# The first two row tiles of x: transposed by a DMA queue instead of by TensorE

## The chip, the core and the metric

The kernel runs on one core of one Trainium2 chip. The metric is the device time of one execution in microseconds (us); lower is better. Three executions of the kernel before are listed, and one more was recorded by the hardware profiler. In that recording PE is TensorE (its weight loads are listed apart as PEld), ACT is ScalarE, DVE is VectorE, POOL is GpSimd, and SP is SyncE, which here only issues DMAs.

## What is computed

```python
def reference(x, w1, b1, w2):          # x 1x2048x512, w1 512x1792, b1 1792, w2 1792x512, all bfloat16
    h = jnp.einsum("bsd,df->bsf", x, w1) + b1
    sp = jnp.log1p(jnp.exp(-jnp.abs(h))) + jnp.where(h > 0, h, jnp.zeros_like(h))
    act = h * jnp.tanh(sp)
    return jnp.einsum("bsf,fd->bsd", act, w2)
```

It is a two-layer dense network with the Mish activation in between: `act(x @ w1 + b1) @ w2`.

## The kernel before

The 2,048 rows of x are worked off in four blocks of 512 rows. For each block a first product (line 177, written `mm1` here) makes h transposed, with one PSUM bank for each tile of 128 columns of w1 (an f tile, 14 of them), and four matmuls for each f tile, one for each 128-wide slice k of the inner dimension. ScalarE applies bias and Mish in one instruction (line 160), writing `a_sb`. The second product (line 199, `mm2`) makes 128 output rows at a time from 14 matmuls; VectorE copies them out of PSUM (line 205) and SP issues the store (line 208). Each engine's instruction order is written out by hand; a `Stream` object inserts a wait for a semaphore only where the engine has not waited for that value yet.

`mm1` needs x with its inner dimension on the partitions, the tile `xT`. The later three blocks get it from a DMA that transposes on its way (the helper `load` with `transpose=True`, line 85). For the first block two ways are used. Row tiles 0 and 1 (256 rows) come by a plain DMA into `x_nat`, row 2p in the first and row 2p+1 in the second half of partition p, and TensorE transposes them against an identity matrix (line 147), eight 128x128 transposes into four PSUM banks. VectorE and ScalarE copy two banks each into `xT` (line 151). GpSimd makes the identity (lines 120 and 122). Row tiles 2 and 3 come by a transposing DMA.

The order of the DMAs is this. ScalarE's queue issues w1's f tiles 0-3 in two halves, k 0-1 and k 2-3 (256 KB each). SP's queue issues `x_nat`, the transposing DMA of tiles 2-3, w1's f tiles 4-7 in two halves, b1, the rest of w1, w2, and the three transposing DMAs of the later blocks. b1 is turned on VectorE (lines 241, 243), and the first Mish waits for it.

Ahead of its work TensorE runs dummy matmuls on constants, whose numbers of columns are in `WARM` (line 130, 3,456 columns in all). Then come the transposes, then `first(...)`, which works on f tiles 0-3 of the first block: tile 0 alone with k 0, tile 1 alone with k 0, both with k 1 to 3, and then row tiles 2-3 with all k. Then `half` runs f tiles 4-7, k 0-1 and k 2-3, with the Mish of f tiles 0-3 queued behind the first half; then f tiles 8 to 13 follow, and the second product of the block.

Since row 2p+j is in column p of tile j, the stores of the first two output tiles go to every second row (`rows`).

Of the kernel before, what the change touches and what calls it, by code (L numbers as in the profile page):

```python
# [4 lines left out]

P = 128
SQ = 32
WARM = (512,) * 5 + (256,) * 3 + (128,)
BLOCKS = (512, 512, 512, 512)


# [21 lines left out]
def bass_standalone__dense_activation_mish__prompt_kernel(  # L33
# [6 lines left out]
):  # L40
    dt = mybir.dt
    ACT = mybir.ActivationFunctionType
    ALU = mybir.AluOpType
    BF, F32 = dt.bfloat16, dt.float32

    _, S, D = x.shape
    F = w1.shape[1]
    KT, FT = D // P, F // P
    assert (S, D, F) == (2048, 512, 1792) and sum(BLOCKS) == S
    x2, out2 = x[0], out[0]  # L50
# [4 lines left out]
    N0 = BLOCKS[0] // P  # L55

    with ExitStack() as es:
        def sb(name, shape, t):
            return es.enter_context(nc.sbuf_tensor(name, shape, t))

        x_nat = sb("x_nat", [P, 2, D], BF)
        xT = sb("xT", [P, KT, S], BF)
        w1_sb = sb("w1_sb", [P, KT, F], BF)
        w2_sb = sb("w2_sb", [P, FT, D], BF)
        b1_nat = sb("b1_nat", [SQ, P], BF)
        b1_T = sb("b1_T", [P, SQ], BF)
        b1_sb = sb("b1_sb", [P, FT], F32)
        ones = sb("ones", [P, P], BF)
        ident = sb("ident", [P, P], BF)
        a_sb = sb("a_sb", [P, FT, S], BF)  # L70
        o_sb = sb("o_sb", [P, S // P, D], BF)
        ps = es.enter_context(nc.psum_tensor("ps", [P, 8, 512], F32))

        def sem(name):
            return es.enter_context(nc.semaphore(name))

        sp = Stream(nc.sync, None)
        pe = Stream(nc.tensor, sem("c_pe"))
        dve = Stream(nc.vector, sem("c_dve"))
        act = Stream(nc.scalar, sem("c_act"))  # L80
        pool = Stream(nc.gpsimd, sem("c_pool"))

        def load(q, dst, src, name, transpose=False):
            s = sem(name)
            (q.eng.dma_start_transpose if transpose else q.eng.dma_start)(dst, src).then_inc(s, 16)
            return (s, 16)
# [8 lines left out]
        def load_part(q, k0, k1, a, b):  # L95
            t = load_w1(q, slice(k0, k1), a, b)
            for f in range(a, b):
                for k in range(k0, k1):
                    t_w1[k, f] = t

        t_bz = dve.mark(nc.vector.memset(b1_nat[:, :], 0.0))  # L101
        for k0, k1 in ((0, 2), (2, 4)):
            load_part(act, k0, k1, 0, F0)
        t_xn = load(sp, x_nat[:, :, :], x2[0:2 * P, :].rearrange("(p j) d -> p j d", p=P), "s_xn")
        t_x23 = load(sp, xT[:, :, 2 * P:4 * P], x2[2 * P:4 * P, :], "s_x23", True)
        for k0, k1 in ((0, 2), (2, 4)):
            load_part(sp, k0, k1, F0, 8)
        sp.wait(t_bz)
# [2 lines left out]
        t = load(sp, w2_sb[:, :, :], w2v, "s_w2")  # L111
# [3 lines left out]
        for s in range(1, len(BLOCKS)):  # L115
            lo, hi = starts[s], starts[s + 1]
            t_xT.append(load(sp, xT[:, :, lo:hi], x2[lo:hi, :], "s_xT%d" % s, True))


        t_ones = pool.mark(pool.eng.memset(ones[:, :], 1.0))  # L120
        pool.wait(t_ones)
        t_id = pool.mark(pool.eng.affine_select(ident[:, :], ones[:, :], pattern=[[1, P]], compare_op=ALU.is_equal,  # L122
                                                fill=0.0, base=0, channel_multiplier=-1))
        act.eng.preload_act_table(ACT.Mish)  # L124

        c_w = nc.const_aps.tensor(1.0, [P, P], BF)
# [2 lines left out]
        def dummy(n):  # L129
            nc.tensor.matmul(ps[:, 7, 0:n], c_w, c_m[:, 0:n], start=True, stop=True)  # L130


        free = [[] for _ in range(8)]
        t_cp = {(j, k): t_x23 for j in (2, 3) for k in range(KT)}
        t_mish, t_acc = {}, {}

        def transpose_x():

            pe.wait(t_xn, t_id)
            for bank, (eng, js, ks) in enumerate(((dve, (0,), (0,)), (act, (1,), (0,)), (dve, (0, 1), (1,)),  # L140
                                                  (act, (0, 1), (2, 3)))):
                n, m = len(ks), len(js)
                psb = ps[:, bank, 0:n * m * P // 2].bitcast(BF)
                for i, k in enumerate(ks):
                    for h, j in enumerate(js):
                        lo = (i * m + h) * P
                        mm = nc.tensor.transpose(psb[:, lo:lo + P], x_nat[:, j, k * P:(k + 1) * P], ident[:, :])  # L147
                eng.wait(pe.mark(mm))
                dst = xT[:, ks[0]:ks[0] + n, js[0] * P:(js[-1] + 1) * P]
                src = psb.rearrange("p (k t) -> p k t", k=n)  # L150
                t = eng.mark(nc.vector.tensor_copy(dst, src) if eng is dve else act.eng.activation(dst, src, ACT.Copy))  # L151
                for k in ks:
                    for j in js:
                        t_cp[j, k] = t
                free[bank] = [t]

        def mish(s, f, bank, t_mm):
            n = BLOCKS[s]
# [6 lines left out]
        def mm1_step(s, f, k, bank, js=None):  # L165

            n = BLOCKS[s]
            lo, hi = (0, n) if js is None else (js[0] * P, (js[-1] + 1) * P)
            first = k == 0 and lo == 0
            if first:  # L170
                pe.wait(*free[bank])
            pe.wait(t_w1[k, f])
            if s:
                pe.wait(t_xT[s])
            else:
                pe.wait(*[t_cp[j, k] for j in (js or range(N0))])
            return nc.tensor.matmul(ps[:, bank, lo:hi], w1_sb[:, k, f * P:(f + 1) * P],  # L177
                                    xT[:, k, starts[s] + lo:starts[s] + hi], start=first, stop=(k == KT - 1 and hi == n))

        def mm1(s, f, bank):  # L180
            for k in range(KT):
                mm = mm1_step(s, f, k, bank)
            mish(s, f, bank, pe.mark(mm))

        s_out = sem("s_out")
        n_out = 0

        def rows(i):

            if i < 2:  # L190
                return out2[0:2 * P, :].rearrange("(p j) d -> p j d", p=P)[:, i, :]
            return out2[i * P:(i + 1) * P, :]

        def mm2_step(i, f, lo, hi, bank):
            s = max(b for b in range(len(BLOCKS)) if starts[b] <= i * P)
# [6 lines left out]
        def put(i, lo, hi, bank, t_mm):  # L202
            nonlocal n_out
            dve.wait(t_mm)
            t = dve.mark(nc.vector.tensor_copy(o_sb[:, i, lo:hi], ps[:, bank, 0:hi - lo]))  # L205
            free[bank] = [t]
            sp.wait(t)
            sp.eng.dma_start(rows(i)[:, lo:hi], o_sb[:, i, lo:hi]).then_inc(s_out, 16)
            n_out += 1

        def mm2(i, lo, hi, bank):
            for f in range(FT):
                mm = mm2_step(i, f, lo, hi, bank)
            put(i, lo, hi, bank, pe.mark(mm))


        def first(js, ks):
            for k in ks:
                for f in range(F0):
                    mm = mm1_step(0, f, k, 4 + f, js)  # L220
                    if k == KT - 1 and js[-1] == N0 - 1:
                        t_acc[f] = pe.mark(mm)

        def half(fs, ks):
            for f in fs:
                for k in ks:
                    mm = mm1_step(0, f, k, f - F0)
                if ks[-1] == KT - 1:
                    t_acc[f] = pe.mark(mm)

        for n in WARM:
            dummy(n)
        transpose_x()
        first((0,), (0,))
        first((1,), (0,))
        first((0, 1), range(1, KT))
        first((2, 3), range(KT))

        dve.wait(t_b1)
        for j in range(P // SQ):  # L240
            t = dve.mark(nc.vector.transpose(b1_T[j * SQ:(j + 1) * SQ, :], b1_nat[:, j * SQ:(j + 1) * SQ]))  # L241
# [52 lines left out]
```

## Time and profile before

| | us |
|---|---|
| three executions, median (lowest to highest) | 105.17 (104.74 to 105.78) |
| the profiled execution, whole | 105.42 |
| its span, from the first instruction to the last | 104.1 |
| TensorE matmuls busy in the span | 101.5 (97%) |
| ScalarE busy | 39.7 (38%) |
| VectorE busy | 12.8 (12%) |

The profiled execution has 1.3 us outside its span. Times in views of the trace count from the span's start. A matmul's recorded duration holds its way through the array, and neighbours overlap; what a matmul costs in a row of matmuls is the distance between two starts.

### The profile page before, as it was taken

What the parts mean: (1) busy time and instruction counts of PE and PEld (TensorE: products, weight loads), DVE (VectorE), ACT (ScalarE), POOL (GpSimd) and SP (SyncE); (2) the same over time, 40 slices, a digit from 0 to 9 for tenths busy, and PEclk for the clock granted to TensorE, in tenths of its full rate; (3) what the DMA queues carried; (4) which work ended last, traced back from release to release, by engine and by line L of the source; (5) the groups of instructions that cost most, each with busy time, mean ns of one, the idle gap of its engine ahead of it and who ended that gap; (6) DMA issues with size and microseconds to landing.
All of it is one profiled execution on the core that took longest, in us unless ns stands there. A gap on an engine that the chain in (4) does not pass through costs nothing.

```text
span 104.1 us, 1139 instructions
## 1 busy us (share of the span) xinstructions
PE 101.5 (97%) x499; PEld 48.8 (47%) x499; DVE 12.8 (12%) x25; ACT 39.7 (38%) x59; POOL 0.7 (1%) x6
## 2 busy tenths in 40 slices
PE   6999999999999999999999999999999999999992
PEld 2786444444444444444444444444444444444462
DVE  0103000022220000022220000022112000011223
ACT  3405997000027777200007777500005777700000
POOL 2000000000000000000000000000000000000000
PEclk9999999999999999999999999999999999999999
DMA  2999999681101000010111000001111000001111
GB/s 46 334 339 363 348 317 178 145 203 50 44 7 50 0 0 6 0 50 0 50 50 50 0 0 3 0 6 50 50 50 50 0 0 0 0 0 57 50 50 50
DMA packets 13345, 7.94 MB, mean 76 GB/s; under 512 B 7836, under 2 KB 13212, under 8 KB 13340
## 3 DMA queue, kind: packets, MB, share of 16 engines
q1 hardware_dynamic: 12796, 7.35, 27.1%
q10 hardware_dynamic: 544, 0.52, 1.4%
q8 instruction: 4, 0.07, 0.3%
q14 instruction: 1, 0.01, 0.0%
HBM read 3.94 MB, written 2.10 MB: 58 GB/s over the span
## 4 chain that ended last, share of the span: by engine, by line
PE 97%; DVE 0%; issue 0%
PE ps L177 47%; PE ps L199 46%; PE ps L130 3%; PE ps L147 1%; DVE o_sb L205 0%
## 5 line engine op out<-in xcount | busy, mean ns | idle before, releaser
L160 ACT ACTIVATE a_sb<-ps,b_sb 128x512 bf16<-128x512 f32 x56 | 37.5, 691 | 48.0 <-PE ps L177 48.0
L177 PE MATMUL ps<-xT,w_sb 128*128 128x512 bf16 (+2 forms) x244 | 49.8, 367 | 0.0
L199 PE MATMUL ps<-w_sb,a_sb 128*128 128x512 bf16 (+2 forms) x238 | 49.0, 366 | 0.0
L177 PEld LDWEIGHTS ps<-xT,w_sb 128*128 128x128 bf16 x244 | 24.2, 101 | 24.8
L199 PEld LDWEIGHTS ps<-w_sb,a_sb 128*128 128x128 bf16 x238 | 22.8, 98 | 25.9
L205 DVE CAST o_sb<-ps 128x512 bf16<-128x512 f32 (+2 forms) x17 | 11.2, 660 | 82.4 <-PE ps L199 82.4
L130 PE MATMUL ps<-const-bfloat16-1.0 128*128 128x512 bf16 (+2 forms) x9 | 3.0, 519 | 0.8 <-PEq L279 0.8
L130 PEld LDWEIGHTS ps<-const-bfloat16-1.0 128*128 128x128 bf16 x9 | 1.2, 138 | 2.3 <-issue 2.2
L124 ACT ACT_TABLE_LOAD x1 | 1.3, 1283 | 1.8 <-issue 1.8
L151 ACT ACTIVATE xT<-ps 128x128 bf16<-128x128 bf16 (+1 forms) x2 | 0.9, 437 | 1.4 <-PE ps L147 1.4
L241 DVE STREAM_TRANSPOSE b_T<-b_nat 32x32 bf16<-32x32 bf16 x4 | 0.8, 202 | 3.3 <-DMA b_nat<-in_b_dram 3.2
L147 PE MATMUL ps<-ident,x_nat 128*128 128x128 bf16 x8 | 1.0, 311 | 0.0
L151 DVE COPY xT<-ps 128x128 bf16<-128x128 bf16 (+1 forms) x2 | 0.5, 258 | 3.2 <-PE ps L147 3.1
L147 PEld LDWEIGHTS ps<-ident,x_nat 128*128 128x128 bf16 x8 | 0.8, 142 | 0.2 <-DMA x_nat<-in_x_dram 0.2
L122 POOL TENSOR_SCALAR_AFFINE_SELECT ident<-ones 128x128 bf16<-128x128 bf16 x1 | 0.3, 292 | 0.1
L101 DVE MEMSET b_nat<- 32x64 uint32 x1 | 0.1, 112 | 0.9 <-PEq L279 0.9
L120 POOL MEMSET ones<- 128x128 bf16 x1 | 0.2, 204 | 0.3 <-POOLq L279 0.3
L243 DVE CAST b_sb<-b_T 128x14 f32<-128x14 bf16 x1 | 0.2, 176 | 0.0
L279 POOL MEMSET const-bfloat16-1.0<- 128x1 bf16 x1 | 0.1, 101 | 0.0
L279 POOL MEMSET const-uint8-127<- 128x1 uint8 x1 | 0.1, 101 | 0.0
L279 POOL MEMSET const-float32-0.0<- 128x1 f32 x1 | 0.1, 98 | 0.3 <-issue 0.3
L279 POOL MEMSET const-float32-1.0<- 128x1 f32 x1 | 0.1, 99 | 0.0
## 6 DMA issues: line engine op xcount, KB each, us to landing
out_dram<-o_sb SPq DMA_DIRECT2D x15, 128.0 KB, 1.7
w_sb<-in_w_dram SPq DMA_DIRECT2D x1, 1792.0 KB, 10.3
w_sb<-in_w_dram SPq DMA_DIRECT2D x1, 768.0 KB, 5.5
w_sb<-in_w_dram ACTq DMA_DIRECT2D x2, 256.0 KB, 3.8
w_sb<-in_w_dram SPq DMA_DIRECT2D x2, 256.0 KB, 4.4
x_nat<-in_x_dram SPq DMA_DIRECT2D x1, 256.0 KB, 2.9
out_dram<-o_sb SPq DMA_DIRECT2D x1, 96.0 KB, 1.6
xT<-in_x_dram SPq DMA_TRANSPOSE x4, 5.9
```

Source lines behind the costliest of these rows:

```text
L120: t_ones = pool.mark(pool.eng.memset(ones[:, :], 1.0))
L122: t_id = pool.mark(pool.eng.affine_select(ident[:, :], ones[:, :], pattern=[[1, P]], compare_op=ALU.is_equal, fill=0.0, base=0, channel_mu ...
L124: act.eng.preload_act_table(ACT.Mish)
L130: nc.tensor.matmul(ps[:, 7, 0:n], c_w, c_m[:, 0:n], start=True, stop=True)
L147: mm = nc.tensor.transpose(psb[:, lo:lo + P], x_nat[:, j, k * P:(k + 1) * P], ident[:, :])
L151: t = eng.mark(nc.vector.tensor_copy(dst, src) if eng is dve else act.eng.activation(dst, src, ACT.Copy))
L160: t = act.mark(act.eng.activation(a_sb[:, f, starts[s]:starts[s + 1]], ps[:, bank, 0:n], ACT.Mish, bias=b1_sb[:, f:f + 1]))
L177: return nc.tensor.matmul(ps[:, bank, lo:hi], w1_sb[:, k, f * P:(f + 1) * P], xT[:, k, starts[s] + lo:starts[s] + hi], start=first, stop=( ...
L199: return nc.tensor.matmul(ps[:, bank, 0:hi - lo], a_sb[:, f, i * P:(i + 1) * P], w2_sb[:, f, lo:hi], start=(f == 0), stop=(f == FT - 1))
L205: t = dve.mark(nc.vector.tensor_copy(o_sb[:, i, lo:hi], ps[:, bank, 0:hi - lo]))
L241: t = dve.mark(nc.vector.transpose(b1_T[j * SQ:(j + 1) * SQ, :], b1_nat[:, j * SQ:(j + 1) * SQ]))
L279: nc = _bacc.Bacc("TRN2", target_bir_lowering=False, num_devices=1)
```

## The change

Row tiles 0 and 1 of x are loaded by a transposing DMA straight into `xT`, as the first transfer of SP's queue; row tiles 2 and 3 by a second one behind it. What served the TensorE way goes: `x_nat`, the identity and its two GpSimd instructions, eight transposes, four copies, the every-second-row stores. The dummies are seven of 512 columns, one of 256 and two of 128 (4,096 columns). Tiles 0 and 1 are no longer taken singly for k 0, so `first((0, 1), range(KT))` has sixteen matmuls of 256 columns, where before eight of 128 and twelve of 256 stood. ScalarE's queue is as before.

```diff
-WARM = (512,) * 5 + (256,) * 3 + (128,)
+WARM = (512,) * 7 + (256,) + (128,) * 2
...
-        t_xn = load(sp, x_nat[:, :, :], x2[0:2 * P, :].rearrange("(p j) d -> p j d", p=P), "s_xn")
-        t_x23 = load(sp, xT[:, :, 2 * P:4 * P], x2[2 * P:4 * P, :], "s_x23", True)
+        t_x = [load(sp, xT[:, :, j * P:(j + 2) * P], x2[j * P:(j + 2) * P, :], "s_x%d" % j, True) for j in (0, 2)]
...
-        t_ones = pool.mark(pool.eng.memset(ones[:, :], 1.0))
-        pool.wait(t_ones)
-        t_id = pool.mark(pool.eng.affine_select(ident[:, :], ones[:, :], pattern=[[1, P]], compare_op=ALU.is_equal,
-                                                fill=0.0, base=0, channel_multiplier=-1))
...
-        t_cp = {(j, k): t_x23 for j in (2, 3) for k in range(KT)}
...
-        def transpose_x():
...
-                pe.wait(*[t_cp[j, k] for j in (js or range(N0))])
+                pe.wait(*[t_x[j // 2] for j in (js or range(N0))])
...
-            sp.eng.dma_start(rows(i)[:, lo:hi], o_sb[:, i, lo:hi]).then_inc(s_out, 16)
+            sp.eng.dma_start(out2[i * P:(i + 1) * P, lo:hi], o_sb[:, i, lo:hi]).then_inc(s_out, 16)
...
-        transpose_x()
-        first((0,), (0,))
-        first((1,), (0,))
-        first((0, 1), range(1, KT))
+        first((0, 1), range(KT))
         first((2, 3), range(KT))
```

More of the change, by code (lines that the diff above doesn't have):

```diff
@@ L42, in bass_standalone__dense_activation_mish__prompt_kernel @@
     ACT = mybir.ActivationFunctionType
-    ALU = mybir.AluOpType
     BF, F32 = dt.bfloat16, dt.float32
@@ L59, in sb @@
             return es.enter_context(nc.sbuf_tensor(name, shape, t))
-        x_nat = sb("x_nat", [P, 2, D], BF)
         xT = sb("xT", [P, KT, S], BF)
@@ L67, in bass_standalone__dense_activation_mish__prompt_kernel @@
         b1_sb = sb("b1_sb", [P, FT], F32)
-        ones = sb("ones", [P, P], BF)
-        ident = sb("ident", [P, P], BF)
         a_sb = sb("a_sb", [P, FT, S], BF)
@@ L80, in bass_standalone__dense_activation_mish__prompt_kernel @@
         act = Stream(nc.scalar, sem("c_act"))
-        pool = Stream(nc.gpsimd, sem("c_pool"))
         def load(q, dst, src, name, transpose=False):
@@ L133, in bass_standalone__dense_activation_mish__prompt_kernel @@
         free = [[] for _ in range(8)]
-        t_cp = {(j, k): t_x23 for j in (2, 3) for k in range(KT)}
         t_mish, t_acc = {}, {}
-        def transpose_x():
[L139 to L155, printed above, removed]
         def mish(s, f, bank, t_mm):
@@ L186, in bass_standalone__dense_activation_mish__prompt_kernel @@
         n_out = 0
[L188 to L192, printed above, removed]
         def mm2_step(i, f, lo, hi, bank):
```

## The prediction

> **What bounds the kernel now.** I read the chain of waits first, in order of time.
>
> ```profile
> 0.80 0.04 issue
> 0.84 3.04 PE ps L130 x9
> 3.88 0.88 PE ps L147 x8
> 4.76 12.89 PE ps L177 x76
> 17.65 12.09 PE ps L199 x56
> 29.74 12.09 PE ps L177 x56
> ...
> 102.31 0.02 issue
> 102.33 0.29 DVE o_sb L205
> ```
>
> The columns are start, length and what ran. TensorE is the chain from 0.84 us to 102.31 us and no DMA stands in it. The end can move only if TensorE's real work starts at another time, runs at another pace, or is held in the middle. So the second view is the first microseconds in order of time (start, length, engine, instruction), and the third a table of windows: length, busy time of TensorE and of its weight loads with their count, and, last, the DMA rate in GB/s.
>
> ```profile
> 3.73 1.03 PE L147 MATMUL ps<-ident,x_nat 128*128 128x128 bf16 x8
> 4.55 0.31 PE L177 MATMUL ps<-xT,w_sb 128*128 128x128 bf16 x1
> ```
>
> ```profile
> 1.75:2.50 0.75, 0.75 (x3) 0.19 (x2) 0.00 (x0) 0.68 (x1) 0.00 (x0) 1.00 0.83 117
> 2.50:3.25 0.75, 0.75 (x4) 0.40 (x3) 0.00 (x0) 0.60 (x1) 0.00 (x0) 1.00 0.98 332
> 3.25:4.25 1.00, 1.00 (x10) 0.71 (x9) 0.20 (x1) 0.09 (x1) 0.00 (x0) 1.00 1.08 378
> 4.25:5.40 1.15, 1.15 (x13) 1.15 (x12) 0.32 (x2) 0.78 (x2) 0.00 (x0) 1.00 1.20 287
> 5.60:6.24 0.64, 0.64 (x6) 0.46 (x4) 0.00 (x0) 0.00 (x0) 0.00 (x0) 1.00 1.10 299
> 7.10:8.85 1.75, 1.75 (x18) 1.57 (x16) 0.82 (x5) 0.00 (x0) 0.00 (x0) 1.00 1.07 373
> 14.50:16.00 1.50, 1.50 (x9) 0.67 (x8) 0.00 (x0) 1.17 (x3) 0.00 (x0) 1.00 1.27 290
> ```
>
> Dummies of 5x512 + 3x256 + 128 = 3,456 columns fill 0.84 to 3.73 us: 0.836 ns a column. The 56 matmuls of 512 columns at 17.65 us take 12.09 us: 0.422 ns a column. TensorE begins at half its later pace. The pace doubles near 6.2 us: before 6.24 three matmuls of 256 columns start in 0.64 us (0.21 us each; the fourth load that the row counts runs in from the left), after 7.10 sixteen in 1.75 us (0.109 us each). I call this the rise of the clock; the granted-clock column shows 1.00 on both sides, so I go by the pace.
>
> That sets the exchange rate. If real work starts d later while the clock is low, it does d/0.836 fewer columns before the rise and pays 0.422 for each of them afterwards: the end moves by 0.5 d. A hole in TensorE after the rise costs its whole length.
>
> **The change part by part.** *Transposes, copies, identity.* Eight transposes hold TensorE from 3.73 to 4.55 us, 0.82 us that go. GpSimd's two instructions and the four copies are on nobody's path then. Merging eight 128-column matmuls into four of 256 leaves the columns as they were, so at the low pace it is worth nothing.
>
> *Dummies.* 4,096 columns at 0.836 ns end at 0.84 + 3.42 = 4.26 us. Real work cannot start before that: 0.29 us earlier than 4.55 at best, a gain of 0.15 us.
>
> *The first transfer.* Real work also needs x tiles 0-1 and w1's first half. Rows of the instructions by tile (duration in ns, start; then the time to landing):
>
> ```profile
> L85 SPq DMA_DIRECT2D x_nat<-in_x_dram x1: 396/396/396, 0.8 to 0.8; - x1
> ...
> DMA to landing us min/median/max: 2.9/2.9/2.9
> ```
>
> ```profile
> L85 SPq DMA_TRANSPOSE xT<-in_x_dram x1: 1305/1305/1305, 1.3 to 1.3; - x1
> ...
> DMA to landing us min/median/max: 4.9/4.9/4.9
> ```
>
> ```profile
> L85 ACTq DMA_DIRECT2D w_sb<-in_w_dram x2: 467/480/494, 0.8 to 1.3; - x2
> ...
> DMA to landing us min/median/max: 3.6/3.8/3.9
> ```
>
> No row shows a transposing DMA at the head of the queue, so I bound it. As quick as `x_nat`, issued at 0.80: 0.80 + 2.9 = 3.7 us. As slow as tiles 2-3 were: 0.80 + 4.9 = 5.7 us. Between them bytes can be counted. Before, four transfers of 0.262 MB were ahead of 5.40 us: the windows from 1.75 give 0.088 + 0.249 + 0.378 + 0.330 = 1.045 MB, that is all four, and tiles 2-3 landed at 1.25 + 4.9 = 6.15, 0.75 us behind their last bytes. They landed last, behind both halves of w1 (0.80 + 3.6 = 4.4, and 1.3 + 3.9 = 5.2), although their issue began earlier than that of w1's second half. If that order holds, with `x_nat` gone, tiles 0-1 are 0.262 MB at 0.37 MB/us earlier than tiles 2-3 were: 6.15 - 0.7 = 5.4 us. If instead they share evenly with w1, they are through when 0.524 MB have moved: 0.337 MB by 3.25 us, the other 0.187 MB at 290 to 378 GB/s by 3.75 to 3.9 us, and 0.75 us of landing: 4.5 to 4.65 us.
>
> The Trainium skill ("DMA: Bandwidth & Descriptors", section "Issuing engines are not separate DMA queues") says that transfers from different engines run on the same 16 DMA engines and interleave with each other. By that rule the shared case holds; the trace speaks against an even share, since there tiles 2-3 came after w1 whole.
>
> I take 4.6 us: the new transfer is issued in the same moment as w1's first half, as `x_nat` was, and that one came ahead of w1; its issue is 0.9 us longer (1,305 against 396 ns), which 3.7 us leaves out. Then real work starts at 4.6 instead of 4.55, with TensorE idle for 0.34 us, and the end moves by 0.02 us. The ends are -0.15 (landing by 4.26) and +0.58 (5.7), if the rise of the clock stays where it is. w1's first half, the other thing awaited, landed at 4.4 with 0.262 MB ahead of it; behind a transfer that is no larger it lands no later than 4.6.
>
> *Tiles 2-3.* They follow on the same queue; alone, a transposing stream runs at 290 GB/s (window 14.50), so 0.9 us for 0.262 MB: 5.5 us, at the far end 6.6. They are needed after sixteen matmuls of 256 columns. From 4.6 these are seven or eight at 0.21 us up to 6.2 and eight or nine at 0.109: 7.1 us. The slack is 0.5 us at the least, as a late first transfer delays the need too.
>
> *What is moved behind.* On SP the long issue is now there twice: 2 x 1.305 us in place of 0.396 + 1.305. Everything behind it issues 0.9 us later: w1's f tiles 4-7, b1, the rest of w1, w2, and the later blocks of x.
>
> ```profile
> L85 SPq DMA_DIRECT2D w_sb<-in_w_dram x1: 568/568/568, 2.6 to 2.6; - x1
> ...
> DMA to landing us min/median/max: 4.3/4.3/4.3
> ```
>
> ```profile
> 7.90 0.90 DVE L241 STREAM_TRANSPOSE b_T<-b_nat 32x32 bf16<-32x32 bf16 x4 [3.24 <-DMA b_nat<-in_b_dram]
> ...
> 9.05 5.89 ACT L160 ACTIVATE a_sb<-ps,b_sb 128x512 bf16<-128x512 f32 x10 [3.65 <-PE ps L177]
> 15.10 0.69 ACT L160 ACTIVATE a_sb<-ps,b_sb 128x512 bf16<-128x512 f32 x1 [0.15 <-PE ps L177]
> ```
>
> w1's part landed at 2.6 + 4.3 = 6.9; 0.9 later is 7.8, and it is needed at 8.85, where f tiles 4-7 begin. b1 arrived at 7.9, and the first Mish ran at 9.05; 0.9 later is 9.95. ScalarE caught up with TensorE only near 15.1, so the delay is handed through eight Mish and more: at 0.69 us each, fourteen from 9.95 end at 19.6 us. Mish f is needed by the second product at 17.65 + 0.216 f (12.09/56 a matmul), the last at 20.46. That leaves 0.8 us; the banks are freed with more. The queues move the same bytes as before, so 0.9 is an upper bound, 0 the lower: cost nothing. If this cover goes, each us beyond it is a whole us. Later blocks of x are needed from 29.74 us, and 0.9 us cannot matter there. The first two stores go to whole rows; their place is off the chain.
>
> Sum: 105.42 - 0.15 to + 0.58, at the taken value +0.02: 105.4 us for an execution like the profiled one. That one was 0.25 us above the median of the runs, so 105.2 us.
>
> **The rivals.** *The clock rises late.* What has to happen before the rise, the trace shows once: TensorE busy without a hole from 0.84 to 6.2 us, 5.4 us. If tiles 0-1 land later than 4.26, a hole opens that was not there. If the hole makes the count start again, the rise comes 5.4 us after the restart: for 5.0 us at 10.4, which is 4.2 us more at the low pace, costing 2.1, plus 0.2 for the start: 107.5. If the count tolerates a part of it, correspondingly less; I put this case at 106.3 to 107.6. It decides where the landing is past 4.26 by more than the count forgives, and I can read no such limit from the trace. For it speaks that tiles 2-3 came last; against it that 0.3 us is a twelfth of the busy stretch.
>
> The Trainium skill ("TensorE: Matmul & The Clock Gate", Part 1) has a rule for it: a free-running window of 4,096 cycles, 3.41 us, in which the array has to be busy. By it the estimate is one window more at half the pace, 1.7 us, and 106.9 to 107.2 us in all. The trace agrees in that the rise at 6.2 is more than 3.41 us after 0.84; it shows no window with a hole.
>
> *Late, but the clock rises all the same.* Tiles 0-1 at 5.0 to 5.7 cost 0.5 x (0.45 to 1.15) = 0.2 to 0.6 us: 105.4 to 105.8.
>
> *Faster.* The transposes weigh less for the clock than full matmuls, and without them the rise comes as early as the end of the dummies, 4.26: 1.9 us less at the low pace, 0.97 + 0.15: 104.1. Against it: the rise came at 6.2 with the transposes in the stretch.
>
> *Held in the middle.* b1 or w1 comes over 0.8 us later than reckoned, because the long issues stall on a full queue: 1 to 2 us, 106.2 to 107.2. Against it: the issue of tiles 2-3 took 1,305 ns with a transfer ahead of it.
>
> **How the numbers follow.** Forecast 0.53, late with the same clock 0.12, clock rises late 0.22, held in the middle 0.04, faster 0.09. 1% is 1.05 us, about what a measurement of this kernel can tell from no change; the runs of before alone spread over 1.04. Within 1% stands 0.53 + 0.12 = 0.65, slower 0.22 + 0.04 = 0.26, faster 0.09. The predicted time is 105.2. For the forecast and the late case together the range is 104.6 to 105.9, the sum's ends with the spread of the runs; it holds 0.65. To leave out no more than 0.2 it has to take in most of the late clock: up to 107.0; below, 104.4 takes in part of the early one.
>
> **What would show it.** In the changed profile the first matmul of line 146 starts between 4.26 and 4.8 us, weight loads wait for `xT` by under 0.5 us, and the pace of 256-column matmuls changes from 0.21 to 0.109 us near 6 us. Matmuls of line 146 and 162 follow with no further idle time, and the first Mish starts between 9.0 and 10.0. The prediction is wrong if tiles 0-1 land after 5 us, if 0.21 us lasts past 8 us, or if a wait for b1 or w1 is in the chain.

## The result and the profile after

| | before | changed |
|---|---|---|
| median of the runs, us | 105.08 (104.74 to 105.78, 4 runs) | 107.89 (107.57 to 108.04, 4 runs) |
| ratio, 95% interval | | 1.0257 (1.0212 to 1.0302) |
| the profiled execution, us | 105.42 | 107.57 |
| its span, us | 104.1 | 106.3 |

The changed kernel is slower by 2.8 us, outside the range of 104.4 to 107.0. In experiments 3, 6, 9 and 12 some runs lie well above the rest; medians hold them, ratios leave them out.

The chain of waits of the changed kernel, in order of time (start, length, what):

```profile
0.73 5.22 DMA xT<-in_x_dram
5.95 0.14 issue
6.09 13.68 PE ps L146 x72
19.77 12.09 PE ps L162 x56
...
104.45 0.29 DVE o_sb L168
```

A transfer now stands in the chain, and it is the one for tiles 0-1: issued at 0.73 us, landed at 5.95. From 19.77 us on each piece is as long as before. So everything that was lost was lost before 19.77 us: the last copy starts at 104.45, before at 102.33, 2.12 us later.

Its first microseconds in order of time:

```profile
3.28 1.06 PE L120 MATMUL ps<-const-bfloat16-1.0 128*128 128x512 bf16 x4
...
6.05 0.77 PEld L146 LDWEIGHTS ps<-xT,w_sb 128*128 128x128 bf16 x5 [1.99 <-issue]
6.09 1.01 PE L146 MATMUL ps<-xT,w_sb 128*128 128x256 bf16 x4 [1.75 <-DMA xT<-in_x_dram]
```

The dummies run out (by their columns at 0.77 + 3.42 = 4.19 us), and TensorE stands idle for 1.9 us until 6.09. Then the windows, with TensorE's busy time, its weight loads and their count, and the DMA rate at the end:

```profile
2.87:3.75 0.88, 0.88 (x4) 0.32 (x3) 0.00 (x0) 0.14 (x1) 0.00 (x0) 1.00 1.25 293
3.75:4.50 0.75, 0.59 (x4) 0.25 (x2) 0.00 (x0) 0.00 (x0) 0.00 (x0) 1.00 1.17 318
6.25:8.75 2.50, 2.50 (x13) 1.76 (x12) 0.24 (x2) 0.00 (x0) 0.00 (x0) 1.00 1.06 339
9.00:10.95 1.95, 1.95 (x20) 1.75 (x18) 0.53 (x3) 0.04 (x1) 0.00 (x0) 1.00 1.06 361
```

From 6.25 to 8.75 twelve matmuls of 256 columns start in 2.50 us, 0.21 us each; after 9.00 eighteen in 1.95, 0.108 each. The clock rises near 9.0 us, in the kernel before it rose near 6.2.

The two facts make up the difference of the two profiled executions. Real work starts at 6.09 instead of 4.55, 1.54 us later, and it is done at half pace for 9.0 - 6.09 = 2.9 us instead of 6.2 - 4.55 = 1.65; half of the 1.25 more is 0.63. 1.54 + 0.63 = 2.17 us against the 2.12 measured. The medians are 2.8 us apart: the profiled execution of the kernel before is 0.3 us above its median, that of the changed kernel 0.3 us below, and where the clock rose in the executions without a profile is not on record. Put as a formula, the last copy starts at: start of real work + 96.95 + half the time at the low pace + waits later on. The constant is set by the kernel before (102.33 - 4.55 - 0.83); it then serves the changed kernel and the experiments below for which it is worked out.

Where tiles 0-1 were held up shows in the packets. The DMA view of 3.75 to 4.50 us (queue q1 is SP's, q10 ScalarE's; packets, MB, share of the engines):

```profile
q10 hardware_dynamic: 185, 0.19, 86.9%
q1 hardware_dynamic: 193, 0.05, 29.6%
```

In this stretch there are as many packets of the one queue as of the other, but those of x have 256 B and those of w1 1,024: x gets a fifth of the bytes, where an even share had been reckoned.

The turns are not all of it. In packets of 256 B tiles 0-1 are 1,024, and from 2.00 to 4.50 us SP's queue moved this many:

```profile
q1 hardware_dynamic: 1014, 0.26, 47.5%
```

If the transfers of one queue go in order, which this view does not show, nearly all of tiles 0-1 was through by 4.50 us. They landed 1.45 us later, where 0.75 us had been reckoned.

### The profile page after: what moved, and what is told of

Same layout as the page of the kernel before. It is cut to its first block, busy times and chain, and to the rows that moved or that the text cites. A ratio compares the mean times of both kernels' runs of the same rounds, so it can differ in the third digit from the quotient of the medians.

```text
span 106.3 us, 1106 instructions
## 1 busy us (share of the span) xinstructions
PE 101.9 (96%) x488; PEld 48.2 (45%) x488; DVE 12.3 (12%) x23; ACT 39.0 (37%) x57; POOL 0.2 (0%) x4
## 4 chain that ended last, share of the span: by engine, by line
PE 93%; DMA 5%; DVE 0%; issue 0%
PE ps L146 47%; PE ps L162 46%; DMA xT<-in_x_dram 5%; DVE o_sb L168 0%
## 5 line engine op out<-in xcount | busy, mean ns | idle before, releaser
L146 PE MATMUL ps<-xT,w_sb 128*128 128x512 bf16 (+1 forms) x240 | 50.4, 373 | 1.7 <-DMA xT<-in_x_dram 1.7
L120 PE MATMUL ps<-const-bfloat16-1.0 128*128 128x512 bf16 (+2 forms) x10 | 3.6, 541 | 0.8 <-PEq L239 0.8
```

## The experiments

My theory after the result had two parts: tiles 0-1 land late because w1's packets go ahead of them and among them, and the hole that this leaves on TensorE postpones the clock. The rivals: the transposing DMA is slow by itself; the clock rises at a time of its own.

**1. Cover the hole.**

```diff
-WARM = (512,) * 7 + (256,) + (128,) * 2
+WARM = (512,) * 12 + (128,)
```

> The changed kernel with 6,272 columns of dummies instead of 4,096, so that TensorE is busy up to the time at which tiles 0-1 landed (5.95 us). Nothing is computed otherwise. Theory 'the hole postpones the clock': tiles 0-1 still land near 5.95 and work starts near 6.1, but the pace doubles between 4.2 and 7.7 us instead of at 8.9, so some 1.0 to 1.3 us come back: 106.3 to 106.9 us. Rival 'only the late start counts, the clock rises at a time of its own': the pace still doubles near 9 us and the time stays at 107.6 to 108.0.

106.30 us (105.79 to 106.40), ratio to the kernel before 1.0108 (1.0046 to 1.0171). In order of time, and a window after the start:

```profile
0.77 4.34 PE L120 MATMUL ps<-const-bfloat16-1.0 128*128 128x512 bf16 x13 [0.77 <-PEq L239]
6.19 0.60 PE L146 MATMUL ps<-xT,w_sb 128*128 128x256 bf16 x4 [1.08 <-DMA xT<-in_x_dram]
```

```profile
6.20:8.05 1.85, 1.85 (x18) 1.66 (x19) 0.00 (x0) 0.00 (x0) 0.00 (x0) 1.00 1.10 336
```

Real work starts at 6.19, no sooner than in the changed kernel, and runs at full pace from its first matmul (19 loads in 1.85 us). In this execution the clock rose so early, near 4 us, that the dummies themselves ended at 5.11 us instead of about 6.0, and left a hole after the rise, which did not bring the low pace back. The dummies alone give back 1.6 us. The formula: 6.19 + 96.95 = 103.14; the last copy started at 103.15.

**2. w1's second half behind tiles 0-1.**

```diff
-        for k0, k1 in ((0, 2), (2, 4)):
-            load_part(act, k0, k1, 0, F0)
-        t_x = [load(sp, xT[:, :, j * P:(j + 2) * P], ..., "s_x%d" % j, True) for j in (0, 2)]
+        load_part(act, 0, 2, 0, F0)
+        t_x = [load(sp, xT[:, :, 0:2 * P], x2[0:2 * P, :], "s_x0", True)]
+        load_part(sp, 2, 4, 0, F0)
+        t_x.append(load(sp, xT[:, :, 2 * P:4 * P], x2[2 * P:4 * P, :], "s_x2", True))
```

> The changed kernel with w1's second half (k 2-3, f tiles 0-3) moved from ScalarE's queue to SP's, between the two transposing DMAs. Theory 'w1 takes the bandwidth': without w1's packets between its own, the first transfer goes through at 250 packets in 0.25 us from 2.85 us and is over by 3.9; it lands at 4.7 to 5.0 instead of 5.95, work starts 1.0 us earlier, the time falls to 106.3 to 107.2. Rival 'a transposing DMA at the head is slow by itself': it lands after 5.6 us, and the time stays above 107.4.

106.69 us (106.53 to 106.84), ratio 1.0157 (1.0109 to 1.0206). The rows of `xT`:

```profile
L80 SPq DMA_TRANSPOSE xT<-in_x_dram x1: 1332/1332/1332, 0.7 to 0.7; - x1
...
DMA to landing us min/median/max: 3.8/3.8/3.8
```

Tiles 0-1 land 3.8 us after their issue at 0.73, at 4.56 us, 1.4 us earlier; in the changed kernel the same row says 5.2. From 2.00 to 4.00 us the packets under 512 B, which are those of tiles 0-1 and a few small ones, are 1,062, so the landing is some 0.56 us behind them. Work starts at 4.70 and, although the dummies had ended at 4.19 as in the changed kernel, at the full pace (eight matmuls of 256 columns in 1.03 us):

```profile
DMA packets 1329, 0.53 MB, mean 267 GB/s; under 512 B 1062, under 2 KB 1329, under 8 KB 1329
```

```profile
4.70 1.03 PE L147 MATMUL ps<-xT,w_sb 128*128 128x256 bf16 x8 [0.38 <-DMA xT<-in_x_dram]
```

The rest of the gain does not arrive: TensorE waits 0.7 us for w1's second half, which now lands at 6.2 us. At the end, SP's own waits show something else:

```profile
SPq L226 <- DMA out_dram<-o_sb: 2.0, 1, 2.0
```

In the kernel before and the changed one this last wait for the stores is 1.1 us. I come back to it in the last section.

**3. Tiles 0-1 alone at the start.** Both of w1's first parts follow tiles 0-1 on SP's queue; ScalarE issues none.

```diff
-        for k0, k1 in ((0, 2), (2, 4)):
-            load_part(act, k0, k1, 0, F0)
...
+        t_x = [load(sp, xT[:, :, 0:2 * P], x2[0:2 * P, :], "s_x0", True)]
+        for k0, k1 in ((0, 2), (2, 4)):
+            load_part(sp, k0, k1, 0, F0)
+        t_x.append(load(sp, xT[:, :, 2 * P:4 * P], x2[2 * P:4 * P, :], "s_x2", True))
```

> The changed kernel with both of w1's first parts moved from ScalarE's queue to SP's, behind the transposing DMA of tiles 0-1, which is then alone at the start. Theory 'w1 takes the bandwidth, and being first in w1's place delays the start of the packets': first packets of x near 1.8 us, landing at 3.8 to 4.4 us; then w1's first half, landing near 4.8 to 5.2, sets the start. Time 106.0 to 107.2. Rival 'slow by itself': first packets of x not before 2.7 us, landing at 4.7 us or later, w1 behind it after 5.3, time above 107.2.

106.85 us (106.01 to 107.77), ratio 1.0146 (1.0076 to 1.0216). Rows by tile, of `xT` and of `w_sb`, and SP's queue from 2.00 to 3.25 us:

```profile
L80 SPq DMA_TRANSPOSE xT<-in_x_dram x1: 1322/1322/1322, 0.7 to 0.7; - x1
...
DMA to landing us min/median/max: 3.1/3.1/3.1
```

```profile
L80 SPq DMA_DIRECT2D w_sb<-in_w_dram x2: 447/507/567, 2.1 to 2.7; - x2
...
DMA to landing us min/median/max: 3.5/3.6/3.7
```

```profile
q1 hardware_dynamic: 1027, 0.26, 89.5%
```

With no other transfer, the transposing DMA lands 3.1 us after its issue, at 3.81 us; plain `x_nat` took 2.9. It is not slow by itself. w1 now lands too late instead, at 2.11 + 3.55 = 5.66 us, and TensorE waits for it. Going from this kernel to experiment 2 adds w1's first half on the other queue and 0.75 us (3.81 to 4.56); from there to the changed kernel, w1's second half and 1.39 us (4.56 to 5.95). So it is w1 on the other queue that makes tiles 0-1 late. By the counts, the packets are through by 3.25 us here, by 4.00 in experiment 2 and by 4.50 in the changed kernel, and the landing comes 0.56, 0.56 and 1.45 us behind them. Of the 1.39 us, then, 0.5 lie among the packets and 0.9 behind them.

**4. A hole in the kernel before.**

```diff
-WARM = (512,) * 5 + (256,) * 3 + (128,)
+WARM = (512,) * 2 + (128,)
```

> The kernel before with 1,152 columns of dummies instead of 3,456: a hole of about 1.9 us ahead of the transposes on TensorE, as long as the one in the changed kernel, while the start of the real work stays at 4.55 us. Theory 'the hole postpones the clock': the pace doubles 0.5 to 3.4 us later than 6.2 us, and the time rises by 0.3 to 1.7 us, to 105.4 to 106.8. Rival 'the clock rises at a time of its own': time stays at 104.8 to 105.4, the pace doubles near 6.2 us.

106.86 us (106.43 to 107.10), ratio 1.0169 (1.0117 to 1.0222). In order of time, and two windows:

```profile
0.84 1.12 PE L130 MATMUL ps<-const-bfloat16-1.0 128*128 128x512 bf16 x3 [0.84 <-PEq L279]
3.84 1.03 PE L147 MATMUL ps<-ident,x_nat 128*128 128x128 bf16 x8 [1.88 <-DMA x_nat<-in_x_dram]
4.67 2.34 PE L177 MATMUL ps<-xT,w_sb 128*128 128x128 bf16 x14
```

```profile
5.45:8.87 3.42, 3.42 (x19) 2.42 (x18) 0.81 (x4) 0.05 (x1) 0.00 (x0) 1.00 1.09 352
9.00:10.50 1.50, 1.50 (x15) 1.25 (x14) 0.08 (x1) 0.30 (x1) 0.00 (x0) 1.00 1.09 354
```

Real work starts at 4.67, as ever, but 18 loads fill 3.42 us up to 8.87, and 14 fill 1.50 after 9.00. The clock rises at 8.9 us, and the kernel loses 1.6 us by nothing but fewer dummies. The formula: 4.67 + 96.95 + (8.9 - 4.67)/2 = 103.74; the last copy started at 103.73. The second part is shown from both sides, by a hole closed and by a hole opened, with nothing but the dummies changed. (The median is 0.06 us above what I had named.)

**5. Experiment 2 with its hole covered.** `WARM = (512,) * 9 + (128,)`.

> The kernel with w1's second half behind tiles 0-1, and dummies of 4,736 columns in place of 4,096, so that TensorE is busy until 4.7 us, when its real work began there. Tiles 0-1 land at 4.6 as before. Theory 'each hole before the rise costs clock': the rise stays between 4.2 and 7.7 us and the time falls by 0 to 0.7 us against 106.7, to 106.0 to 106.7. Rival 'a hole of 0.56 us is forgiven': no change, 106.5 to 106.9. In both the waits of 0.7 us for w1's second half and 0.2 us for tiles 2-3 remain.

106.58 us (106.49 to 106.69), ratio 1.0141 (1.0097 to 1.0186), against 106.69: no change. The time does not show by itself that the hole was forgiven: w1's second half lands at 6.3 us, TensorE waits for it whatever the pace was until then, and so the start is covered by a later wait. The profile of experiment 2 shows it, by the full pace from 4.70 us on.

**6. w1's second half in smaller packets.**

```diff
-        for k0, k1 in ((0, 2), (2, 4)):
-            load_part(act, k0, k1, 0, F0)
+        load_part(act, 0, 2, 0, F0)
+        for f in range(0, F0, 2):
+            load_part(act, 2, 4, f, f + 2)
```

> The changed kernel with w1's second half on ScalarE's queue as two transfers of two f tiles each, so that its packets have 512 B instead of 1,024. Theory 'the two queues take turns packet by packet, so 256 B of x stand against 1,024 B of w1': the share of x in the stretch of both rises from a fifth to a third, tiles 0-1 land 0.2 to 0.6 us earlier than 5.95, at 5.35 to 5.75, time 107.3 to 107.8. Rival 'the two share by bytes or by another rule': landing at 5.8 to 6.1 us, time as in the changed kernel, 107.6 to 108.0.

Six of ten runs are at 105.64 to 106.07 us, four at 107.44 to 107.88; ratio of the lower ones 1.0075 (1.0047 to 1.0102). The packets from 3.75 to 4.00 us:

```profile
q10 hardware_dynamic: 97, 0.05, 76.0%
q1 hardware_dynamic: 93, 0.02, 44.1%
```

Again as many packets of the one as of the other; with 512 B against 256, x has a third of the bytes. Tiles 0-1 land 4.7 us after their issue, at 5.42 us, 0.53 earlier than in the changed kernel. The two levels I had not expected, and the lower one is far below the 107.3 to 107.8 us that I had expected from the earlier landing. The profiled execution is one of the upper ones; of the lower ones there is no profile. In it real work starts at 5.56, 1.4 us after the dummies, and the pace changes only near 10 us:

```profile
7.00:9.00 2.00, 2.00 (x12) 1.44 (x10) 0.36 (x2) 0.00 (x0) 0.00 (x0) 1.00 1.05 357
10.00:12.00 2.00, 2.00 (x16) 1.46 (x15) 0.00 (x0) 0.88 (x2) 0.00 (x0) 1.00 1.10 357
```

**7 and 8. Smaller holes in the kernel before.** `WARM = (512,) * 5 + (256,) + (128,)` and `(512,) * 4 + (128,) * 2`.

> The kernel before with 2,944 columns of dummies instead of 3,456: a hole of 0.4 us ahead of the transposes, start of the real work unchanged. Theory 'a window of activity in which most must be busy': a hole of 0.4 us is forgiven, 104.9 to 105.5 us. Rival 'any hole makes the count start again': as in the hole of 2 us, 106.4 to 107.1 us.

> The kernel before with 2,304 columns of dummies instead of 3,456: a hole of 1.0 us ahead of the transposes. Theory 'a window in which most must be busy': between the hole of 0.4 and that of 2 us, 105.2 to 106.4. Rival 'any hole makes the count start again': 106.4 to 107.1 us, the same as with 0.4 and with 2 us.

| dummy columns | hole in the profiled execution, us | median, us | ratio |
|---|---|---|---|
| 3,456 (before) | 0 | 105.1 | 1 |
| 2,944 | 0.3 | 105.13 | 1.000 (0.997 to 1.003) |
| 2,304 | 0.9 | 106.38 | 1.012 (1.008 to 1.015) |
| 1,152 (experiment 4) | 2.0 | 106.86 | 1.017 (1.012 to 1.022) |

A hole of 0.3 us costs nothing, one of 0.9 us most of what one of 2 us costs; with 106.38 it stands on the border between my theory and its rival. What the clock forgives here, behind 1.9 to 2.5 us of dummies, lies between the two. Experiments 3 and 9 show that this is not a limit for every hole.

**9. ScalarE's table load ahead of w1.**

```diff
+        act.eng.preload_act_table(ACT.Mish)
         for k0, k1 in ((0, 2), (2, 4)):
             load_part(act, k0, k1, 0, F0)
...
-        act.eng.preload_act_table(ACT.Mish)
```

The dummies are 4,480 columns.

> The changed kernel with ScalarE's table load (1.28 us) ahead of its two loads of w1 instead of behind them, so that they issue at 2.0 and 2.5 us, and dummies of 4,480 columns, up to 4.5 us. Theory 'w1's packets ahead of and among those of x made tiles 0-1 late': tiles 0-1 land at 3.8 to 4.2 us as when alone, w1's first half behind them at 4.4 to 4.8, its second at 5.3 to 6.0; work starts at 4.5 to 4.8 and the time is 105.0 to 105.9 us. Rival 'the two transposing DMAs in a row are what is slow': tiles 0-1 land after 5 us and the time stays above 106.5.

106.33 us (106.11 to 108.11), ratio 1.0153 (1.0132 to 1.0174). The edit did not do what it was for:

```profile
0.72 1.28 ACT L97 ACT_TABLE_LOAD   x1 [0.72 <-PEq L238]
0.75 0.95 ACTq L80 DMA_DIRECT2D w_sb<-in_w_dram  x2
```

The DMAs are issued at 0.75 us beside the table load. Tiles 0-1 land at 5.88, as in the changed kernel. It says nothing of the rivals about the transfers, but a good deal about the clock. A window after the start of real work, of this kernel and then of experiment 3:

```profile
6.05:7.90 1.85, 1.85 (x18) 1.65 (x19) 0.00 (x0) 0.00 (x0) 0.00 (x0) 1.00 1.04 307
```

```profile
5.80:7.30 1.50, 1.50 (x15) 1.34 (x15) 0.00 (x0) 0.00 (x0) 0.00 (x0) 1.00 1.05 231
```

Both work at 0.1 us a weight load, the full pace, although TensorE had stood idle for 1.5 us just before: here from 4.52 (0.77 + 3.75) to 6.01, in experiment 3, with the dummies of the changed kernel, from 4.19 to 5.71. (The formula without a low pace: 6.01 + 96.95 = 102.96; the last copy started at 102.98.) In experiment 6 the same dummies and a hole of 1.4 us left the low pace until near 10 us. So the length of the hole does not decide alone. These holes follow 3.4 to 3.7 us of dummies, those of experiments 7 and 8 only 1.9 to 2.5; and behind 3.4 us both outcomes occur (experiments 3 and 6); what decides between them is not shown.

**10. Experiment 6 with its hole covered.** `WARM = (512,) * 11`.

> The changed kernel with w1's second half in packets of 512 B, as before, and with dummies of 5,632 columns, up to 5.5 us, when its real work began there. Theory 'the hole decides by chance whether the clock rises one window later': the runs near 107.7 us are gone, all are at 105.3 to 106.1. Rival 'the two levels have another cause, in the DMAs': both levels remain, 105.6 to 106.1 and 107.4 to 107.9.

106.34 us (106.18 to 106.47, 4 runs), ratio 1.0149 (1.0128 to 1.0169). The upper level is not there, which fits the chance theory but is thin: four runs against ten, and they lie above the lower level of experiment 6, not at it. Tiles 0-1 landed at 5.62 in its profile.

**11 and 12. Two attempts at a version that beats both.** In 11, w1's second half goes behind both x transfers, and TensorE does k 0-1 for all rows first. The diff of 11 is against the kernel of experiment 5. In 12, the second half stays on ScalarE's queue, but ScalarE waits for the fourth dummy before it issues it; the dummies are 4,736 columns there too.

```diff
-        load_part(sp, 2, 4, 0, F0)
         t_x.append(load(sp, xT[:, :, 2 * P:4 * P], x2[2 * P:4 * P, :], "s_x2", True))
+        load_part(sp, 2, 4, 0, F0)
...
-        first((0, 1), range(KT))
-        first((2, 3), range(KT))
+        for ks in ((0, 1), (2, 3)):
+            first((0, 1), ks)
+            first((2, 3), ks)
```

```diff
-        for k0, k1 in ((0, 2), (2, 4)):
-            load_part(act, k0, k1, 0, F0)
+        load_part(act, 0, 2, 0, F0)
+        act.wait((pe.sem, 1))
+        load_part(act, 2, 4, 0, F0)
...
-        for n in WARM:
-            dummy(n)
+        for i, n in enumerate(WARM):
+            mm = dummy(n)
+            if i == 3:
+                pe.mark(mm)
```

> The kernel with w1's second half behind both x transfers on SP's queue, dummies of 4,736 columns, and TensorE's order changed to fit: k 0-1 for tiles 0-1, then for tiles 2-3, then k 2-3 for both. Theory 'what is left over the kernel before is waiting for transfers in the order in which TensorE asks for them': tiles 0-1 land near 4.5, tiles 2-3 near 5.6, w1's second half near 6.5; holes after the start of 0.5 us or less instead of 1.0, time 105.2 to 106.2 us. Rival 'the transposing DMAs cost more than that whatever the order': 106.4 us or more.

> The changed kernel with w1's second half still on ScalarE's queue, but issued only when the fourth dummy is done (near 2.7 us), and dummies of 4,736 columns. Theory 'w1's packets among those of x made tiles 0-1 late': x goes through before w1's second half begins, tiles 0-1 land at 4.4 to 4.8, the second half at 5.3 to 6.2, work starts near 4.7 us and the time is 105.0 to 106.0 us. Rival 'two queues at work delay the landing, whenever the other one's packets come': tiles 0-1 land after 5.2 us, time above 106.2.

107.30 us (106.57 to 107.71), ratio 1.0191 (1.0141 to 1.0241), and 106.45 us (106.16 to 108.38), ratio 1.0123 (1.0082 to 1.0164). Neither beats the kernel before. In 11 tiles 0-1 land at 4.74, although the second transposing DMA stands right behind the first as in the changed kernel; so two of them in a row, the rival of experiment 9, do not make tiles 0-1 late. TensorE starts at 4.87, but w1's second half lands at 8.0 us and not at 6.5:

```profile
3.65 4.37 DMA w_sb<-in_w_dram
8.02 0.05 issue
8.07 10.55 PE ps L147 x56
```

In 12 the packets of tiles 0-1 do go through before w1's second half (from 2.00 to 4.00 us there are 1,104 packets under 512 B), and they still land at 5.21, 1.2 us later; w1's second half lands at 7.36. A window table of 12 shows when:

```profile
2.85:4.00 1.15, 1.15 (x4) 0.44 (x3) 0.00 (x0) 0.86 (x1) 0.00 (x0) 1.00 1.23 275
4.00:6.25 2.25, 1.78 (x8) 0.82 (x7) 0.00 (x0) 0.42 (x1) 0.00 (x0) 1.00 0.86 104
6.25:7.25 1.00, 0.82 (x5) 0.34 (x3) 0.00 (x0) 0.00 (x0) 0.00 (x0) 1.00 1.23 289
```

For 2.25 us all queues together move 104 GB/s, with work on both. My theory of packets taking turns does not give that; in 12 landing (5.21, by a hair) and time are the rival's. So w1 on the other queue delays tiles 0-1 in two ways: by turns among the packets (experiment 6), and by something that acts behind their own packets, which is not found.

## Why the prediction was wrong

**The landing of the first transfer** is the step that failed. The prediction took 4.6 us with 5.7 as the far end; it landed at 5.95. Both terms of the 4.6 were too small: the packets were to be through by 3.75 to 3.9 us and were by 4.5, and the landing was to come 0.75 us behind them and came 1.45 behind. The argument for 4.6 was that the transfer, issued in the same moment as w1's first half, would come ahead of w1 as `x_nat` had. It came behind: w1's first half landed at 3.53 us, before it had been 4.4, and x's packets began near 2.8. The longer issue is the likely reason: alone, in experiment 3, x's first packets go at 2.1 us, while w1's first go at 1.8 in the changed kernel; that the issue decides was not tried by itself. And the even share that gave 4.5 to 4.65 was counted in bytes, where the queues took turns in packets of unequal size. The lateness behind the packets stays unexplained; it is there in experiment 12 too. The far end itself, "as slow as tiles 2-3 were", was no bound, because their packets went when those of the other queue were nearly through.

**The exchange rate** held. 0.5 us for each us of later start at the low pace, a full us otherwise, explains every profile for which it is worked out here (the changed kernel, experiments 1, 4 and 9) to 0.05 us.

**"If the rise of the clock stays where it is"** was the second condition, and it failed with the first. The hole was 1.9 us, not 0.34. The rival "the clock rises late" had the mechanism and the sign, and 107.5 for a landing at 5.0; measured 107.89 for one at 5.95. Its size came out nearly right by two errors: the start was a us later than in its example, and the clock needed only 2.9 us after the restart, not 5.4. Those 5.4 us, read from one row, were no fixed count: in experiment 1 the clock rose near 4 us, 3.2 us after the first dummy. I gave it 0.22, because 0.3 us had seemed a twelfth of the busy stretch; with a hole of that length this was right (experiment 7), but the landing decided the hole. Whether a hole of 1.4 to 1.9 us behind these dummies costs the clock seems to be in part chance: the changed kernel and experiment 6 lost by it in their profiles, experiment 3 did not. The Trainium skill's window of 3.41 us ("TensorE: Matmul & The Clock Gate", Part 1) came nearer than my count from one row in how much later the clock rises: 3.41 us by the window and 4.2 by my count, and the rise came 2.8 us later than before. The time by it, estimated at 106.9 to 107.2 us, was too low. Its window fits here only if it need not be busy throughout, as the 2.9 us after the hole are less than 3.41.

**What went as reckoned.** The transposing stream ran at 293 GB/s (290 reckoned). The later issues on SP hid: b1's turning began at 8.48 us, 0.6 later than before (0 to 0.9), and no wait for it or for w1 is in the chain. That the cost of the eight transposes goes is true as well: 0.82 us of TensorE were removed, and a wait of 1.9 us took their place.

## What to carry to other kernels

A transfer that is moved to the head of its queue is not at the head of the DMA engines: ask what the other queue issues in the same microsecond, and compare the packet sizes, because the queue with the smaller packets got the smaller share of the bytes here. Dummy work that keeps a clock up is part of the same schedule as the transfer that it bridges; when the transfer moves, the dummies have to follow: a hole of 0.9 us behind 1.9 us of dummies cost 1.3 us through the clock alone, while two profiles passed a hole of 1.5 us behind 3.4 and 3.7 us of dummies without loss. Transposes on an engine that would otherwise idle are cheap (here w1's first half landed only at 4.4 us, while they ran), and removing them gains only what the data's arrival allows.

## What the runs showed of the hardware that was not expected

Two queues took turns by packets: 185 against 193 with 1,024 and 256 B, 97 against 93 with 512 and 256 B. The Trainium skill ("DMA: Bandwidth & Descriptors", section "Queues, rings and completion order") has the engines go round between queues at packet granularity; the counts agree if its packets are the ones that the trace lists.

Behind a transposing stream the queues went slowly for a while. The rates are 104 GB/s for 2.25 us in experiment 12, and in experiment 3, from the window view, 85 GB/s just behind tiles 0-1:

```profile
2.00:3.25 1.25, 1.25 (x4) 0.45 (x3) 0.00 (x0) 0.01 (x1) 0.00 (x0) 1.00 0.89 207
3.25:4.00 0.75, 0.75 (x4) 0.38 (x3) 0.00 (x0) 0.00 (x0) 0.00 (x0) 1.00 0.61 85
```

In the changed kernel all queues together moved 54 GB/s from 5.25 to 5.50 us, just ahead of the landing of tiles 0-1. In the kernel before, where w1 came first, no such stretch delays it. The cause stays open; so does the related one, why tiles 0-1 in the changed kernel land 1.45 us after nearly all of their packets.

In experiments 2, 5 and 11 the last store took 0.8 to 1.0 us longer (2.0, 1.9 and 2.1 us of SP's last wait against 1.1). In the DMA view of the last 2.3 us of experiment 2 an instruction fetch stands beside the store:

```profile
q1 hardware_dynamic: 288, 0.13, 19.4%
q14 instruction: 1, 0.01, 0.8%
```

Such a fetch falls at this place in the three profiles and in none of the others. That it delays the store was not tried. Their times hold some 0.9 us that is not the price of the order of transfers.
